# A gated mix of sliding attention and a token MLP on Trainium2: when the first two W2 loads are issued

## The chip, the cores and the metric

The kernel runs on one core of one Trainium2 chip. The metric is the device time of one execution in microseconds (us), taken as the median of several runs. A profiled execution has a time of its own, and its span, from the first to the last instruction of the program, is somewhat shorter than that.

The engines are named as the profile names them: PE (TensorE, matrix multiplications; PEld is its weight load), DVE (VectorE), ACT (ScalarE), POOL (GpSimd) and SP (SyncE, which here only issues transfers). A "q" behind a name, as in SPq, is the sequencer of that engine, where transfers are issued and semaphores are waited for. Every transfer runs on the core's 16 DMA engines. In the profile's table of queues, q1 carries the transfers issued by SP, q10 those by ACT and q0 those by POOL.

## The reference

The inputs are bf16. One token sequence `A_x` of 2048 x 512 goes through two branches that a gate mixes:

```
q, k, v = x @ wqkv                 # 32 heads of 16
a = softmax(q . k[s - 0, 2, .., 14] / 4) . v[s - 0, 2, .., 14] @ wo
h = layernorm(x)
u = gelu(h^T @ w1 + b1)            # contracts 2048 tokens, 1792 features F
b = (u @ w2 + b2)^T                # contracts F, back to 2048 tokens
g = sigmoid(sum(x * gate_w))
out = g * a + (1 - g) * b
```

W1 is 2048 x 1792 and W2 is 1792 x 2048. Both go through the core once.

## The kernel before

Everything lives in one SBUF tensor, `arena`, that is cut into named regions. Regions are used again by other data once their first data is dead, so a load into such a region must wait until the last reader is through.

**The planner.** The kernel does not write its instructions down in order. It collects operations with estimated durations, with the named resources that each reads and writes, and with two kinds of ties to other operations. `deps` is a real dependence: the operation waits until the other has finished, and for a load that means until it has landed. `after` is a tie of order only: the operation comes after the other is issued. A list scheduler (`_pass`) then picks an order for each engine, by earliest possible start and then by the length of the chain of work behind an operation, and `plan_waits` puts a semaphore wait in front of an operation wherever a dependence is not already known to be met. All of this happens when the kernel is built; on the chip each engine runs its list in order, and an instruction that waits holds everything behind it on its own engine.

**The stages on PE.** First the q, k and v projections (L586, L645). Then "phase 2", `ph2_<ft>_<half>` (L853): for each of 14 tiles of 128 features, two halves of eight 512-column matmuls that contract the tokens with W1; GELU on ACT writes the result to `UT`. Two small groups of the attention scores, `sum0` and `sum1` (L709, L714), are placed between them. Then "phase 3", `ph3_<i>_<half>` (L880): for each of 16 output tiles, two halves of seven matmuls with W2, and four more with the attention output and `wo` (L889, five tiles behind). The output tiles are evacuated by ACT (L448, the last half by DVE at L929) and stored by SP (L902, L932).

**The attention beside it.** DVE forms the products of queries and keys and sums them up (L445), with some sums done by accumulating transfers on the POOL queue (L739, L822). After the softmax of each half of the tokens, POOL issues four transfers of 512 KB that spread the attention weights over the partitions, `av0_0` to `av0_3` for the first half and `av1_0` to `av1_3` for the second (L782).

**The weight loads.** All go out on SP through the helper `load`, so all of them stand at L487. W1 comes in seven loads of 1024 KB, `w1_0` to `w1_6`, each for two feature tiles, into three slots that are used in turn (`W1W`, resources `w1s0` to `w1s2`). Load `w1_j` waits until PE has finished with `w1_(j-3)`: `w1_6` goes out when feature tile 7 is done, and feature tile 12 is the first that needs it. W2 comes in eight loads of 896 KB, `w2_0` to `w2_7`, each for two output tiles. They take dead regions: `w2_0` and `w2_1` lie side by side in the region `XT` (the transposed input), `w2_2` to `w2_4` in the W1 slots, `w2_5` and `w2_6` in `X`, and `w2_7` in small softmax buffers. `W2ALIAS[j]` (L370) names the resources that load j overwrites; the helper counts them as written, so a load waits for their readers and for whoever wrote them last.

Two of these ties matter here. The eight loads are chained by `after`, each behind the one before it, and `w2_0` behind `w1_6`; so the SP list goes on `w1_6, w2_0, w2_1, ... w2_7`, and then come the output stores. And `w2_0` and `w2_1` both name all of `XT` (`XTALL`) as written, although each fills its own part of it. Since `w2_0` is then the last writer of `XTALL`, `w2_1` has `w2_0` as a dependence: SP waits until `w2_0` has landed before it issues `w2_1`.

On PE, `ph2_12_0` waits for `w1_6`, `ph3_0_0` for `w2_0`, `ph3_2_0` for `w2_1`, `ph3_4_0` for `w2_2`, and so on. Phase 3 begins with an order written out by hand, `head` (L908): the first halves of tiles 0, 1 and 2, then their second halves.

Of the kernel before, what the change touches and what calls it, by code (L numbers as in the profile page):

```python
# [307 lines left out]
def bass_gated_mix__sliding_local_dilated__mixer_token_mlp__prompt_kernel(nc, A_x, A_wqkv, A_wo, B_x, B_w1, B_b1, B_w2, B_b2, gate_w, out, dbg=None):  # L308
    with contextlib.ExitStack() as es:
# [54 lines left out]
        def w2view(name, extra=0):  # L364
            return view(name, BF16, [(256, NFT), (1, 256)], extra=extra)

        XTALL = ["xt0_%d_%d" % (t, k_) for t in range(4) for k_ in range(2)] + ["xt1", "xt2", "xt3"]
        W2S = [w2view("XT"), w2view("XT", NFT * 256), w2view("W1", NST * 256), w2view("W1", 2 * NST * 256), w2view("W1"),
               w2view("X"), w2view("X", NFT * 256), w2view("S4")]
        W2ALIAS = [XTALL, XTALL, ["w1s1"], ["w1s2"], ["w1s0"],  # L370
                   ["x%d" % t for t in range(7)], ["x%d" % t for t in range(7, 14)], ["s4", "s2", "s1", "rs", "rb"]]
        assert 4 * UT_ * 4 + 2 * UT_ * 4 + 2 * UT_ * 4 + UT_ * 2 >= NFT * 256 * 2
        WO = view("WO", BF16, [(D, 4), (1, D)])
# [104 lines left out]
        w1ld = {}  # L478
        late_dep = [[]]

        def load(name, dst, src, nbytes, writes, transpose=False, queue="sp", issue=0.5, order=True, deps=(), after=()):
            ds = sch.dsem(name)

            def fn(e):
                if transpose:
                    return e.dma_start_transpose(dst, src)
                return e.dma_start(dst, src)  # L487
            op = sch.dma(queue, fn, nbytes, ds, issue=issue, writes=writes, deps=list(deps) + late_dep[0],
                         after=list(after) + ([last_ld[queue]] if order and queue in last_ld else []), name=name)
            if order:  # L490
                last_ld[queue] = op
            return op
# [37 lines left out]

        def ld_w2(j):
            w1ld[7 + j] = load("w2_%d" % j, W2S[j], w2v[:, :, 256 * j:256 * j + 256], F * 256 * 2, ["w2_%d" % j] + W2ALIAS[j], order=False,
                               after=[w1ld[6 + j]])

        ld_w1(0)

# [331 lines left out]
        for j in range(8):  # L868
            ld_w2(j)
# [144 lines left out]
```

## Time and profile before

| | |
|---|---|
| median of 4 runs | 168.63 us (168.23 to 168.94) |
| the profiled execution, own time | 168.23 us |
| its span | 166.5 us |
| PE busy | 160.8 us, 97% of the span, 817 matmuls |
| DVE busy | 150.9 us, 91% |
| ACT busy | 75.2 us, 45% |
| TensorE clock granted | full in all slices |
| bytes moved by DMA | 32.11 MB; q1 21.96 MB, q0 9.45 MB |

How to read it: PE and DVE both have little idle time. An engine's busy share is an average over the stages, so what a change in one place is worth has to be read from the waits in that place. A "time to landing" runs from the issue of a transfer to the last of its 16 semaphore increments, one from each DMA engine that carries a share of it.

### The profile page before, as it was taken

The numbers are of one execution on the slowest core, as the hardware profiler recorded it, in microseconds if no ns is written. First come the engines' busy times: TensorE is split into PE (matmuls) and PEld (weight loads), VectorE is DVE, ScalarE is ACT, GpSimd is POOL, SyncE is SP. The second block draws the span as 40 slices with busy tenths as digits, with TensorE's granted clock in tenths as the row PEclk, the third lists the DMA queues.
The fourth block names the chain that finished last, engine by engine and source line by source line (L and its number), as shares of the span: only waits on it lengthen the run. The fifth ranks groups of instructions, "written<-read, shape, count | busy, mean of one in ns | idle before, by whom it ended". The sixth has DMA issues, their size and how long they took to land.

```text
span 166.5 us, 2019 instructions
## 1 busy us (share of the span) xinstructions
PE 160.8 (97%) x817; PEld 78.7 (47%) x817; DVE 150.9 (91%) x126; ACT 75.2 (45%) x104; POOL 13.7 (8%) x38
## 2 busy tenths in 40 slices
PE   7999999999999999999999599999999999999993
PEld 2765555555544444444444244444444444444742
DVE  0399999999999999999999996999999999999931
ACT  3356677766682799762111639410022211111164
POOL 7000002020000000005000000005001221000000
PEclk9999999999999999999999999999999999999999
DMA  5999997729597082768997749999996899971014
GB/s 167 325 233 265 198 320 134 129 47 189 141 292 218 4 248 60 196 187 136 187 253 247 217 113 303 290 290 290 224 365 230 169 217 184 210 176 37 32 55 134
DMA packets 44120, 32.11 MB, mean 193 GB/s; under 512 B 7248, under 2 KB 41680, under 8 KB 44112
## 3 DMA queue, kind: packets, MB, share of 16 engines
q1 hardware_dynamic: 40800, 21.96, 49.5%
q0 software_dynamic: 2608, 9.45, 27.7%
q10 hardware_dynamic: 704, 0.59, 1.1%
q8 instruction: 6, 0.10, 0.2%
q14 instruction: 2, 0.02, 0.0%
HBM read 18.88 MB, written 2.10 MB: 126 GB/s over the span
## 4 chain that ended last, share of the span: by engine, by line
PE 86%; DMA 10%; POOL 1%; issue 0%; DVE 0%; POOLq 0%
PE ps L880 29%; PE ps L645 23%; PE ps L853 21%; DMA arena<-in_B_w_dram 10%; PE ps L889 8%; PE ps L586 3%; POOL arena L487 1%; PE ps L567 1%; PE ps L709 1%; PE ps L714 1%; PE ps L558 0%; DVE arena L929 0%; POOL arena L455 0%; PE ps L794 0%; POOL arena L454 0%
## 5 line engine op out<-in xcount | busy, mean ns | idle before, releaser
L445 DVE TENSOR_TENSOR arena<-arena 128x4096 bf16<-128x4096 bf16 (+8 forms) x79 | 132.0, 1720 | 2.2 <-ACT arena L448 1.2
L853 PE MATMUL ps<-arena 128*128 128x512 bf16 x224 | 49.0, 379 | 1.8 <-DMA arena<-in_B_w_dram 1.8
L880 PE MATMUL ps<-arena 128*128 128x512 bf16 (+1 forms) x238 | 50.2, 367 | 0.0
L448 ACT ACTIVATE arena<-ps,arena 128x512 bf16<-128x512 f32 (+1 forms) x30 | 21.7, 728 | 61.6 <-PE ps L889 41.5
L448 ACT ACTIVATE arena<-ps 128x512 bf16<-128x512 f32 (+3 forms) x53 | 32.9, 629 | 19.2 <-PE ps L645 11.1
L645 PE MATMUL ps<-arena 128*128 128x512 bf16 x176 | 38.3, 379 | 0.0
L880 PEld LDWEIGHTS ps<-arena 128*128 128x128 bf16 x238 | 23.3, 98 | 25.3
L853 PEld LDWEIGHTS ps<-arena 128*128 128x128 bf16 x224 | 21.7, 98 | 28.4 <-issue 2.7
L645 PEld LDWEIGHTS ps<-arena 128*128 128x128 bf16 x176 | 19.9, 113 | 17.7
L889 PE MATMUL ps<-arena 128*128 128x512 bf16 (+1 forms) x68 | 15.6, 367 | 0.0
L949 ACT ACT_TABLE_LOAD x11 | 14.1, 1283 | 2.5 <-issue 2.3
L782 POOL DMA_DIRECT2D arena<-arena x8 | 4.3, 561 | 75.3 <-DVE arena L445 75.3
L889 PEld LDWEIGHTS ps<-arena 128*128 128x128 bf16 x68 | 6.7, 98 | 7.2
L684 DVE BATCH_NORM_STATS2 arena<-arena 128x6 f32<-128x512 bf16 x16 | 9.8, 683 | 0.0
L448 ACT ACTIVATE arena<-arena 128x16 f32<-128x16 f32 (+5 forms) x10 | 6.8, 679 | 5.7 <-DVE arena L445 5.6
L579 DVE COPY arena<-ps 128x256 bf16<-128x256 bf16 x4 | 1.1, 292 | 5.1 <-PE ps L567 5.1
L698 DVE TENSOR_SCALAR arena<-arena 128x512 bf16<-128x512 bf16 x16 | 5.5, 418 | 0.0
L822 POOL DMA_DIRECT2D arena<-arena x3 | 3.6, 1200 | 19.0 <-DVE arena L445 19.0
L739 POOL DMA_DIRECT2D arena<-arena x2 | 2.5, 1234 | 29.4 <-DVE arena L695 20.7
L929 DVE TENSOR_SCALAR arena<-ps,arena 128x256 bf16<-128x256 f32 x1 | 0.5, 545 | 4.4 <-PE ps L889 4.4
L586 PE MATMUL ps<-arena 128*128 128x256 bf16 x32 | 4.5, 297 | 0.0
L586 PEld LDWEIGHTS ps<-arena 128*128 128x128 bf16 x32 | 3.5, 119 | 1.0 <-DVE arena L579 0.7
(39 smaller groups left out, 20.4 us busy)
## 6 DMA issues: line engine op xcount, KB each, us to landing
arena<-in_B_w_dram SPq DMA_DIRECT2D x7, 1024.0 KB, 6.0
arena<-in_B_w_dram SPq DMA_DIRECT2D x8, 896.0 KB, 10.0
arena<-arena POOLq DMA_DIRECT2D x5, 1024.0 KB, 8.2
arena<-arena POOLq DMA_DIRECT2D x8, 512.0 KB, 13.1
out_dram<-arena SPq DMA_DIRECT2D x15, 128.0 KB, 2.0
arena<-in_A_x_dram SPq DMA_DIRECT2D x3, 512.0 KB, 4.9
arena<-in_A_wqkv_dram SPq DMA_DIRECT2D x2, 512.0 KB, 4.3
arena<-in_A_wo_dram SPq DMA_DIRECT2D x1, 512.0 KB, 9.3
```

Of the source, the lines that this page charges most:

```text
L445: return lambda e: e.tensor_tensor(out=o_, in0=a_, in1=b_, op=op_)
L448: return lambda e: e.activation(out=o_, in_=i_, func=f_, **kw)
L586: ins = e.matmul(ps[:, dl, hb * 256:hb * 256 + 256], lhsT=sub(WQKV, dt * 3 * D + dl, [(4, 128)]), rhs=XT[:, dt, hb * 256:hb * 256 + 256], ...
L645: ins = e.matmul(ps[:, bank, :], lhsT=sub(WQKV, dt * 3 * D + tn * D + dl, [(4, 128)]), rhs=XT[:, dt, sb * 512:(sb + 1) * 512], start=(dt = ...
L684: A("dve", (lambda t_: lambda e: e.bn_stats(out=ST6[:, t_, :], in_=X[:, t_, :]))(t), 0.67, reads=["x%d" % t], writes=["st%d" % t], name="s ...
L698: A("dve", (lambda t_: lambda e: e.tensor_scalar(out=X[:, t_, :], in0=X[:, t_, :], scalar1=col(RSTD, t_), scalar2=col(NMR, t_), op0=ALU.mu ...
L782: prev = sch.dma("pool", (lambda d_, s_: lambda e: e.dma_start(d_, s_))(dst, src), 524288, sch.dsem("av%d_%d" % (h, c)), issue=1.0, reads= ...
L822: sch.dma("pool", (lambda o_, i_: lambda e: e.dma_start(o_, i_, accum_op=ALU.add, max_dma_last_dim=4096))(pw(0, 4), pw(4, 4)), 1800000, sc ...
L853: ins = e.matmul(ps[:, bank, :], lhsT=W1W[:, (ft // 2) % 3, st, 128 * (ft % 2):128 * (ft % 2) + 128], rhs=X[:, st, :], start=(st == 0), st ...
L880: ins = e.matmul(ps[:, bank, 0:c1 - c0], lhsT=W2S[i // 2][:, ft, 128 * (i % 2):128 * (i % 2) + 128], rhs=UT[:, ft, c0:c1], start=(ft == 0) ...
L889: ins = e.matmul(ps[:, bank, 0:c1 - c0], lhsT=OT[:, i // 2, dl, 128 * (i % 2):128 * (i % 2) + 128], rhs=WO[:, dl, c0:c1], start=False, sto ...
L949: e.preload_act_table_set(want)
```

## The change

`w2_0` gets a dependence on `w1_6`: SP issues it only when the last W1 load has landed. `w2_1` no longer names `XTALL` as written, so it has no dependence on `w2_0` any more and is tied to it by order alone: SP issues it right behind `w2_0`. That the old contents of `XT` are dead is still ensured, since `w2_0` is issued after `w1_6`, which waits for feature tile 7 on PE.

```
-        W2ALIAS = [XTALL, XTALL, ["w1s1"], ["w1s2"], ["w1s0"],
+        W2ALIAS = [XTALL, [], ["w1s1"], ["w1s2"], ["w1s0"],
                    ["x%d" % t for t in range(7)], ["x%d" % t for t in range(7, 14)], ["s4", "s2", "s1", "rs", "rb"]]
...
         def ld_w2(j):
             w1ld[7 + j] = load("w2_%d" % j, W2S[j], w2v[:, :, 256 * j:256 * j + 256], F * 256 * 2, ["w2_%d" % j] + W2ALIAS[j], order=False,
-                               after=[w1ld[6 + j]])
+                               after=[w1ld[6 + j]], deps=[w1ld[6]] if j == 0 else [])
```

No instruction is added or removed on any engine but the waits; no transfer changes its size, its source or its destination.

## The prediction

> **What bounds the kernel now.** I read the engine table first, then the chain of waits around the loads, then who waits for whom on PE and SP, then every load by itself in narrow windows, then the DMA traffic by stage.
>
> The page's first line of the engine table:
>
> ```profile
> PE 160.8 (97%) x817; PEld 78.7 (47%) x817; DVE 150.9 (91%) x126; ACT 75.2 (45%) x104; POOL 13.7 (8%) x38
> ```
>
> PE is busy for all but 5.7 of 166.5 us. The change touches only the one late place where PE stands still, which the chain of waits shows (start us, us, what):
>
> ```profile
> 62.44 15.55 PE ps L853 x72
> 78.00 0.02 issue
> 78.01 16.43 DMA arena<-in_B_w_dram
> 94.44 0.14 issue
> 94.57 7.07 PE ps L853 x32
> 101.64 18.13 PE ps L880 x84
> ```
>
> The load issued at 78.01 is `w1_6`; it lands at 94.44, 16.43 us later, and PE takes up feature tile 12 0.13 us after that. Tiles 12 and 13 take 7.07 us, and phase 3 begins at 101.64. What PE lost is in the waits of PE (us in total, times, longest), and what SP waited for between the loads in the waits of SP:
>
> ```profile
> PE ps L853 <- DMA arena<-in_B_w_dram: 1.8, 1, 1.8
> SPq L487 <- DMA arena<-in_B_w_dram: 7.8, 1, 7.8
> ```
>
> The first line is the whole price of the late `w1_6`: 1.8 us. The second is `w2_1` waiting for `w2_0` to land. Next, L487 in narrow windows (one issue's ns three times over, start, then time to landing): `w1_5`; `w1_6` with `w2_0`; `w2_1`; `w2_2`:
>
> ```profile
> L487 SPq DMA_DIRECT2D arena<-in_B_w_dram x1: 368/368/368, 71.1 to 71.1; - x1
> DMA to landing us min/median/max: 5.6/5.6/5.6
> ...
> L487 SPq DMA_DIRECT2D arena<-in_B_w_dram x2: 367/5604/10841, 78.0 to 78.4; - x2
> DMA to landing us min/median/max: 16.4/17.5/18.6
> ...
> L487 SPq DMA_DIRECT2D arena<-in_B_w_dram x1: 367/367/367, 97.0 to 97.0; - x1
> DMA to landing us min/median/max: 5.4/5.4/5.4
> ...
> L487 SPq DMA_DIRECT2D arena<-in_B_w_dram x1: 697/697/697, 97.5 to 97.5; - x1
> DMA to landing us min/median/max: 8.2/8.2/8.2
> ```
>
> A W1 load in a quiet stretch lands after 5.6 us. `w1_6` took 16.4, with `w2_0` issued 0.4 us behind it; that issue stood on SP for 10.84 us, until 89.2. `w2_1` landed in 5.4 us although `w2_2` was issued 0.4 us behind it, and `w2_2` followed at 105.7, some 3.2 us later. So loads of one queue don't share the engines evenly: the first is not slowed, the second comes one transfer later. What slowed `w1_6` is the other queue: four `av0` transfers of 512 KB, issued by POOL from 75.3 to 77.5. Three of them, then the DMA by stage (window, busy time of each engine, clock, DMA share, GB/s):
>
> ```profile
> L782 POOL DMA_DIRECT2D arena<-arena x3: 551/561/566, 75.9 to 76.9; - x3
> DMA to landing us min/median/max: 9.0/13.1/14.3
> ```
>
> ```profile
> 76.00:79.00 3.00, 3.00 (x16) 1.37 (x14) 3.00 (x2) 0.69 (x1) 1.49 (x3) 1.00 0.81 95
> 80.00:83.00 3.00, 3.00 (x16) 1.35 (x15) 3.00 (x2) 0.69 (x1) 0.00 (x0) 1.00 0.93 175
> 91.00:93.00 2.00, 1.77 (x20) 0.52 (x18) 2.00 (x1) 0.86 (x2) 0.00 (x0) 1.00 1.10 323
> 102.00:112.00 10.00, 10.00 (x48) 4.48 (x47) 9.77 (x8) 4.22 (x6) 0.00 (x0) 1.00 1.19 290
> ```
>
> The engines are busy but move only 95 to 175 GB/s while `av0` is under way, and 323 once it is over, at 91.27 (76.9 + 14.3).
>
> **What the Trainium skill says.** "DMA: Bandwidth & Descriptors", section "Queues, rings and completion order": each DMA engine goes round the queues that have work, packet by packet, and takes one queue's descriptors in ring order. The trace agrees: `w2_1` with `w2_2` behind it is not slower than a lone load, and `w1_6` beside `av0` is nearly three times slower. The same page, "Anatomy of one DMA — SWDGE (gpsimd) path": engines don't wait on semaphores, the issuing sequencer does; a transfer (of the POOL path, for which the figure is given) has a fixed part of about 2.0 us. The trace, for SP's path: 5.4 us for one load against 3.16 from landing to landing in the run of W2 loads, so about 2.2 fixed. That is the price of a restart.
>
> **The change part by part.** All times are of the profiled execution: span 166.5, own time 168.23, which is 0.40 below the median of 168.63.
>
> *1. `w2_0` waits for `w1_6`.* The SP list behind it holds `w2_1` to `w2_7` and the stores; none can be issued in the meantime. The issue moves from 78.38 to 94.44 + 0.03 (SP's reaction: `w2_0`'s last increment came at 97.03, `w2_1` went out at 97.05) = 94.47. At 5.40 us, which `w2_1` of the same size took from a standstill, it lands at 99.87 instead of 97.03. PE needs it at 101.64, less 0.13 of reaction: 1.6 us to spare. The cover is feature tiles 12 and 13, 7.07 us that begin with the very landing that releases SP, so it moves along if `w1_6` is earlier or later; 5.4 + 0.1 fits. Cost 0.
>
> *2. `w2_1` right behind.* It goes out at about 94.9 and lands one transfer, 3.16 us, after `w2_0`: 103.03, against 102.45 now. PE needs it at `ph3_2_0`, two half tiles of 1.51 us into phase 3, at 104.66: 1.5 to spare. Cost 0. SP's wait of 7.8 us goes, and its place is taken by one of some 5 us for `w1_6` (89.2, when the issue of `w2_0` now ends, to 94.4), plus the 10.8 of that issue.
>
> *3. The later loads.* All shift by 103.03 - 102.45 = 0.6 us at most. `w2_2` lands at 106.3 and is needed at 101.64 + 9.07 (head) + 3.02 (tile 3) = 113.7; `w2_3` at 109.4, needed at 120.6. `w2_4` stays tied to the end of tile 13 and to the queue ahead of it. `w2_7` waits for DVE in any case (3.0 us of SP wait at 113.2), which swallows the rest. The first store is due on SP at 121.5, long after. Cost 0.
>
> *4. What `w1_6` gains.* Upper bound first: the whole stall, 1.80. But `w2_0`'s issue stood until 89.2, so its bytes can't have moved much before about 90. In the records of semaphore increments the 16 shares of `w1_6` land from 88.14 to 94.44, those of `av0_3` from 85.70 to 91.27 and those of `w2_0` from 94.10 to 97.03. The last engine of `w1_6` thus ended 3.17 us after the last engine of `av0_3`. One engine's share of `w1_6` is 1 MB / 16 = 65.5 KB; at 323 / 16 = 20.2 GB/s that takes 3.2 us. So on the engine that decides, `w1_6` was starved by `av0` and then ran at full pace, with `w2_0` already on the others: nothing is left for `w2_0` to have cost there. It could only have slowed `av0` between 89.3 and 91.3, and at half pace that would be 1.0 us. Lower bound: below 0 is excluded, since no traffic is added ahead of `w1_6`. I take 0.1 and keep 0 to 1.0.
>
> *5. Order.* `w2_1` stays behind `w2_0` by its tie of order, so the chains that the planner weighs keep their lengths; PE's list is fixed by hand but for `sum0`, `sum1` and `t_e`, which need no W2; DVE and ACT work before phase 3 needs none either. I count no reordering.
>
> *Sum:* -0.1 us: 168.1 for the profiled execution, 168.5 for the median. About 0.5% (0.84 us) is what a measurement of this kernel can tell from no change.
>
> **The rivals.**
> *A, faster: `w2_0` does hold up `w1_6`.* For it: they are issued together and land 2.6 us apart, and PE waits for just this. Against it: the full pace above, and `w2_1`'s undisturbed 5.4. If so, all of the 1.80 can go: feature tile 12 starts at 92.77. DVE doesn't cap this; its attention work ends at 159.45 and the matmuls that need it come at 162.1, 2.6 later, and its own wait for ACT (1.2 us) would shrink too. 168.63 - 1.80 = 166.8; half of it, by slowed `av0`, gives 167.6. It decides for faster from 0.84 us on. Chance 0.08.
>
> *B, slower: the two W2 loads share the engines.* With both starting from nothing, and packets of both interleaved, `w2_0` would land with `w2_1`, at 103.03, and PE would stand from 101.64 to 103.17: +1.5 us, 170.1. It costs from a landing time of 7.07 us on, and shows as slower from 7.9. Against it: `w2_1` and `w2_2` were in the same position and came one after the other. Chance 0.06.
>
> *C: the change doesn't do what it says.* Were `w2_1` still to wait for `w2_0`, it would go out at 99.9 and land at 105.3, and PE would lose 105.3 + 0.13 - 104.66 = 0.8 us at `ph3_2_0`: 169.4. By the code no dependence is left. Chance 0.02.
>
> **How the numbers follow.** My forecast, no change within 0.5%, has 0.84. Faster is A, 0.08; slower is B and C together, 0.08 (C's 0.8 us stands at the bound and is counted here). Predicted 168.5. Noise of the median is about 0.3 to each side (the runs span 168.23 to 168.94); the gain's bound of 1.0 pulls the lower end to 167.7, and a C-like loss the upper one to 169.3. The rest of A and B lies outside.
>
> **What would show it.** Right: `w2_0` issued within 0.1 us of `w1_6`'s landing, at about 94.4 and landing in 5.4; `w2_1` 0.4 behind, landing 8.2 after its issue; SP's wait for a load changed in place; PE's wait at L853 still 1.7 to 1.8 us, with none at L880; phase 3 from 101.6. Wrong: a landing time of `w1_6` under 15 us with PE's wait gone (A), or a PE wait for a load at L880 (B, C).

## The result and the profile after

| | before | after |
|---|---|---|
| median | 168.66 us (64 runs) | 168.51 us (43 runs) |
| ratio of after to before, 95% interval | | 1.0004 (0.9987 to 1.0020) |
| profiled execution, own time / span | 168.23 / 166.5 us | 169.39 / 167.6 us |

The time did not change measurably. A second comparison gave 1.0022 (0.9996 to 1.0049). Runs more than 1.5% above the fastest of the same kernel are left out of the ratios. The two profiled executions of the changed kernel (169.39, and 169.49 in the second one) both lie above its median, so what they show in excess of 166.5 us is not the typical run.

The chain of waits of the changed kernel around the loads (start us, us, what), and then the waits of PE and of SP (us in total, times, longest):

```profile
62.42 15.55 PE ps L853 x72
77.98 0.02 issue
77.99 16.49 DMA arena<-in_B_w_dram
94.48 0.14 issue
94.62 3.63 PE ps L853 x16
```

```profile
PE ps L853 <- DMA arena<-in_B_w_dram: 1.9, 1, 1.9
PE ps L541 <- POOL arena L454: 1.1, 1, 1.1
PE ps L889 <- DVE arena L445: 0.6, 1, 0.6
```

```profile
SPq L487 <- DMA arena<-in_B_w_dram: 16.1, 1, 16.1
```

`w1_6` still took 16.49 us, although no transfer stood behind it on its queue any more, and PE's wait at L853 is 1.9 us where it was 1.8. SP's long wait is the new one, for `w1_6`. The loads after the change, in narrow windows of L487: `w1_6`, then `w2_0`, then `w2_0` and `w2_1` together.

```profile
L487 SPq DMA_DIRECT2D arena<-in_B_w_dram x1: 368/368/368, 78.0 to 78.0; - x1
DMA to landing us min/median/max: 16.5/16.5/16.5
...
L487 SPq DMA_DIRECT2D arena<-in_B_w_dram x1: 368/368/368, 94.5 to 94.5; - x1
DMA to landing us min/median/max: 7.1/7.1/7.1
...
L487 SPq DMA_DIRECT2D arena<-in_B_w_dram x2: 368/594/821, 94.5 to 94.9; - x2
DMA to landing us min/median/max: 7.1/8.5/9.9
```

`w2_0` went out at the landing of `w1_6`, as expected, but took 7.1 us, not 5.4. It landed at 101.62; PE took it up at 101.75, with less than 0.1 us of idle time at L880. So the cover of tiles 12 and 13 held, with nothing to spare.

### The profile page after: what moved, and what is told of

Same layout as the page of the kernel before. It is cut to its first block, busy times and chain, and to the rows that moved or that the text cites. A ratio compares the mean times of both kernels' runs of the same rounds, so it can differ in the third digit from the quotient of the medians.

```text
span 167.6 us, 2019 instructions
## 1 busy us (share of the span) xinstructions
PE 160.9 (96%) x817; PEld 78.1 (47%) x817; DVE 151.1 (90%) x126; ACT 75.2 (45%) x104; POOL 13.7 (8%) x38
## 4 chain that ended last, share of the span: by engine, by line
PE 37%; DVE 29%; DMA 22%; SPq 7%; ACT 2%; issue 1%
DVE arena L445 29%; PE ps L853 19%; PE ps L645 16%; DMA arena<-in_B_w_dram 10%; DMA arena<-arena 7%; SPq L486 6%; DMA arena<-in_A_x_dram 5%; ACT arena L448 2%; SPq L487 1%; PE ps L889 1%; ACT L949 1%; PE ps L709 1%; PE ps L714 1%; DVE arena L929 0%; PE ps L794 0%
## 5 line engine op out<-in xcount | busy, mean ns | idle before, releaser
L853 PE MATMUL ps<-arena 128*128 128x512 bf16 x224 | 49.0, 379 | 1.9 <-DMA arena<-in_B_w_dram 1.9
L880 PE MATMUL ps<-arena 128*128 128x512 bf16 (+1 forms) x238 | 50.2, 367 | 0.1
L645 PE MATMUL ps<-arena 128*128 128x512 bf16 x176 | 38.5, 379 | 0.3 <-DMA arena<-in_A_x_dram 0.3
L880 PEld LDWEIGHTS ps<-arena 128*128 128x128 bf16 x238 | 23.1, 98 | 25.8 <-issue 0.5
L853 PEld LDWEIGHTS ps<-arena 128*128 128x128 bf16 x224 | 21.7, 98 | 28.5 <-issue 2.8
L949 ACT ACT_TABLE_LOAD x11 | 14.1, 1283 | 2.5 <-issue 2.3
L586 PE MATMUL ps<-arena 128*128 128x256 bf16 x32 | 4.0, 274 | 0.0
L541 PE MATMUL ps<-arena 128*128 128x512 bf16 x5 | 2.3, 628 | 1.1 <-POOL arena L454 1.1
## 6 DMA issues: line engine op xcount, KB each, us to landing
arena<-in_B_w_dram SPq DMA_DIRECT2D x8, 896.0 KB, 10.1
```

The source lines that it names most:

```text
L586: ins = e.matmul(ps[:, dl, hb * 256:hb * 256 + 256], lhsT=sub(WQKV, dt * 3 * D + dl, [(4, 128)]), rhs=XT[:, dt, hb * 256:hb * 256 + 256], ...
L645: ins = e.matmul(ps[:, bank, :], lhsT=sub(WQKV, dt * 3 * D + tn * D + dl, [(4, 128)]), rhs=XT[:, dt, sb * 512:(sb + 1) * 512], start=(dt = ...
L853: ins = e.matmul(ps[:, bank, :], lhsT=W1W[:, (ft // 2) % 3, st, 128 * (ft % 2):128 * (ft % 2) + 128], rhs=X[:, st, :], start=(st == 0), st ...
L880: ins = e.matmul(ps[:, bank, 0:c1 - c0], lhsT=W2S[i // 2][:, ft, 128 * (i % 2):128 * (i % 2) + 128], rhs=UT[:, ft, c0:c1], start=(ft == 0) ...
L949: e.preload_act_table_set(want)
```

## The experiments

**The theory** was that the four `av0` transfers of POOL hold up `w1_6`, that `w2_0` has no part in it, and that the added wait lies under tiles 12 and 13. **Rival A**: `w2_0` shares the blame. **Rival B**: two W2 loads in flight slow each other. "Ratio" is always to the kernel before on the same chip, with its 95% interval.

**1. The changed kernel again.**

> The changed kernel again, for a second profile beside the kernel before on the same chip. Theory (the POOL transfers av0 hold w1_6 up, w2_0 has no part in it; the wait is covered by feature tiles 12 and 13): w1_6 still takes about 16.4 us to land, PE still waits 1.7 to 1.9 us at L853; w2_0 goes out within 0.1 us of that landing and lands 5.1 to 5.5 us later, with 1 us or more to spare before phase 3; time 0.0 +- 0.3 us against before. Rival A (w2_0 shares in holding up w1_6): w1_6 lands in under 15.5 us, PE's wait under 1 us, 1 to 1.8 us faster. Rival B (the two W2 loads share the engines and are late): a PE wait for a load at L880 of about 1.5 us, 1.5 us slower.

Ratio 1.0022 (0.9996 to 1.0049). `w1_6` took 16.9 us and PE waited 2.3 us at L853 (tile 11 had ended earlier in this execution). `w2_0` landed 6.6 us after its issue, at 101.02. No wait at L880. A and B both miss; the space before phase 3 was 0.5 us, not the 1 us that I had asked for.

**2. The alias alone.** The other edit is left out:

```
-        W2ALIAS = [XTALL, XTALL, ["w1s1"], ...
+        W2ALIAS = [XTALL, [], ["w1s1"], ...
```

> One half of the change alone: w2_1 no longer names XTALL, w2_0 still goes out right behind w1_6. So three loads stand in SP's queue while av0 is under way. Theory (loads of one queue are served in order): w1_6 lands after 16.4 us as before, w2_0 about 2.6 us behind it at 97.0, w2_1 about 3 us behind that, near 100.1 instead of 102.4; PE's wait at L853 1.7 to 1.9 us; time 0.0 +- 0.3 us. Rival A: with one more load beside it, w1_6 lands later than 17 us and PE waits over 2.4 us, 0.6 us slower or more.

Ratio 1.0008 (0.9986 to 1.0031). `w1_6` 16.7 us with two loads behind it, `w2_0` at 97.5, `w2_1` at 100.5; PE's wait 2.1 us. Two loads queued behind `w1_6` don't slow it by more than single executions scatter: with nothing behind it, it took 15.3 to 16.9 us in five of them.

**3. The wait alone.** `w2_0` waits for `w1_6`, and `w2_1` still waits for `w2_0`:

```
-                               after=[w1ld[6 + j]])
+                               after=[w1ld[6 + j]], deps=[w1ld[6]] if j == 0 else [])
```

> The other half alone: w2_0 waits for w1_6 to land, and w2_1 still waits for w2_0 to land. This is rival C of the prediction made real. Theory: w2_0 lands at 99.9, w2_1 goes out then and lands 5.4 us later at 105.3; PE needs it at 104.66, so a new PE wait of 0.6 to 0.9 us stands at L880 and the time is 0.6 to 0.9 us above before. Rival D (the space of 1.5 us behind w2_1 is larger than the modelled matmul ends suggest, or a restart costs less than 2.2 us): no wait at L880, time unchanged.

I was right about the place and wrong about the size. Two of six runs came out near 170 (169.86 and 171.09), the other four at 176.6 to 179.3; the median of all six is 177.21, 5.3% above before (168.34). The ratio of 1.0147 (1.0080 to 1.0215) counts only the two near 170. What decides between the two outcomes was not tried, but the long times have a cause in the kernel: the next experiment has them in every run. The waits of PE in one of the long runs here:

```profile
PE ps L880 <- ACT arena L448: 7.2, 1, 7.2
PE ps L880 <- DMA arena<-in_B_w_dram: 1.7, 1, 1.7
```

The second line is the wait that I expected, for `w2_1` (landed at 105.37). The first, four times as long, was in nobody's expectation.

**4. A longer wait.** The changed kernel, with `w2_0` held until feature tile 12 is done:

```
-                ... deps=[w1ld[6]] if j == 0 else [])
+                ... deps=[w1ld[6], ph2op[12, 1]] if j == 0 else [])
...
-                PE(f_ph2(ft, bank, half), 1.735, ...
+                ph2op[ft, half] = PE(f_ph2(ft, bank, half), 1.735, ...
```

> The changed kernel with the wait made longer: w2_0 waits for w1_6 and also for the end of feature tile 12 on PE, some 3.6 us after the landing; w2_1 right behind it. Measures the space that the change has. Theory: w2_0 goes out at about 98.2 and lands at 103.6; PE needs it at 101.6, so PE waits about 2.1 us at L880; w2_1 lands at 106.8 and is needed 3.0 us after phase 3 begins at 103.7, so it costs nothing or 0.2 more. Time 1.9 to 2.4 us above before, about 170.7. Rival B (the loads share the engines): both land at about 106.8, a PE wait of about 5 us at L880, time about 173.8.

Ratio 1.0582 (1.0524 to 1.0640), median 178.26: nearly five times the cost that I expected. The loads themselves did what they should (`w2_0`, then `w2_1`, in windows of L487):

```profile
L487 SPq DMA_DIRECT2D arena<-in_B_w_dram x1: 368/368/368, 98.3 to 98.3; - x1
DMA to landing us min/median/max: 5.2/5.2/5.2
...
L487 SPq DMA_DIRECT2D arena<-in_B_w_dram x1: 822/822/822, 98.7 to 98.7; - x1
DMA to landing us min/median/max: 7.9/7.9/7.9
```

`w2_0` landed 5.2 us after its issue and `w2_1` 3.2 us behind it: B is out. The rest is in the waits of PE and ACT, and in the first store (L902):

```profile
PE ps L880 <- ACT arena L448: 6.1, 1, 6.1
PE ps L880 <- DMA arena<-in_B_w_dram: 1.9, 1, 1.9
```

```profile
ACT arena L448 <- DMA out_dram<-arena: 15.9, 1, 15.9
```

```profile
L902 SPq DMA_DIRECT2D out_dram<-arena x1: 5127/5127/5127, 127.2 to 127.2; - x1
...
who waited for it (us, times):
  ACT arena L448: 15.9, 1
...
DMA to landing us min/median/max: 24.0/24.0/24.0
```

Then `w2_7`, the load ahead of this store on SP, and last the same store in the kernel before:

```profile
L487 SPq DMA_DIRECT2D arena<-in_B_w_dram x1: 11111/11111/11111, 116.0 to 116.0; - x1
...
DMA to landing us min/median/max: 34.8/34.8/34.8
```

```profile
L902 SPq DMA_DIRECT2D out_dram<-arena x1: 361/361/361, 121.5 to 121.5; - x1
...
DMA to landing us min/median/max: 7.7/7.7/7.7
```

Read from below. The store of output tile 0 went out at 127.2 (before: 121.5) and landed 24.0 us later (before: 7.7). ACT's evacuation of tile 4 writes the same output buffer, since the ring has four, so it waited 15.9 us for that landing. PE needs a PSUM bank (a part of the memory that the matmuls write to) that this evacuation frees, and waited 6.1 us. The store was late twice over because it stood behind `w2_7`. On SP, the issue of `w2_7` lasted from 116.0 for 11.1 us. On the queue, `w2_7` landed at 150.80, 34.8 us after its issue (before: 14.1), and the store 0.36 us behind it, at 151.16; from about 113 on POOL's `av1` and then its accumulating transfers were under way. And there is a third part, in the clock row of the page (one digit for each fortieth of the span):

```profile
PEclk9999999999999999999999999999999998589999
```

With PE's stop the granted clock fell: it was 0.79 from 145.5 to 152.0, mostly the stop itself, and 0.61 from 152.0 to 157.2. (The clock records have half the full clock from 149.25 to 156.08.) The 14 matmuls after the stop took 5.15 us; 14 such matmuls take 3.02 in the chain of the kernel before, so 2.1 us were lost. The parts sum to 1.9 + 6.1 + 2.1 = 10.1 us, and the span is 176.8 - 166.5 = 10.3 longer.

**5. The same, with eight output buffers.** To tell whether the ring of four is what makes it so dear:

```
-            A("act", act(OUTS[:, i % 4, :], ...
+            A("act", act(OUTS[:, i % 8, :], ...
```

The stores, their semaphores and the resources go with it in the same way; the buffers take the room of two dead softmax buffers and one new slot.

> The kernel whose w2_0 waits until feature tile 12 is done (5.8% above before, where 1.2% was expected), with eight output buffers in the ring instead of four (in the room of two dead softmax buffers and one new slot), so that ev4 no longer waits for the store of tile 0. Theory (the late W2 loads push w2_7 and the first stores behind it into the accumulating transfers of POOL; the store of tile 0 lands some 24 us late; the ring of four makes ACT and then PE wait for it, and PE loses its clock on top): the store of tile 0 still lands late, near 150, but ACT doesn't wait for it before tile 8; PE's wait of 6 us for ACT and the granted clock of 0.98 are gone; PE's wait of 1.9 us for w2_0 stays; time 1.0 to 2.0% above before, 170 to 171.5. Rival (the extra time comes from elsewhere, such as a slower PE after the wait for w2_0): still 4% or more above before.

Ratio 1.0131 (1.0089 to 1.0172), median 170.12. The waits of PE, and the first store:

```profile
PE ps L880 <- DMA arena<-in_B_w_dram: 2.0, 1, 2.0
PE ps L853 <- DMA arena<-in_B_w_dram: 1.8, 1, 1.8
PE ps L541 <- POOL arena L454: 1.1, 1, 1.1
```

```profile
L902 SPq DMA_DIRECT2D out_dram<-arena x1: 11065/11065/11065, 128.1 to 128.1; - x1
...
DMA to landing us min/median/max: 24.2/24.2/24.2
```

The store is as late as before, 24.2 us, and now nobody waits for it: ACT's wait for a store, PE's wait for ACT and the lower clock are all gone, and what is left is the wait for `w2_0`. So it is the ring of four that turns the late store into the extra 8 us (medians of 178.26 and 170.12, on two chips on which the kernel before has 168.34 and 168.09).

**6. `av0` out of the way.** The kernel before, with one wait more on POOL and no other edit: `av0_1`, and in order `av0_2` and `av0_3`, go out only when `w1_6` has landed. The wait is put in after planning, so no order changes (`avop` is a list that collects the four transfers as they are made):

```
-        sch.plan_waits()
+        sch.plan_waits(); avop[0][1].waits.append(w1ld[6])
```

> The kernel before, with one wait more on POOL: av0_1 (and in order av0_2 and av0_3 behind it) goes out only when w1_6 has landed. av0_0 alone stays ahead. Takes away three quarters of the suspected cause. Theory (av0 starves w1_6): w1_6 waits for av0_0 alone and lands after 6 to 8 us, at about 85, PE's wait of 1.8 us at L853 is gone and tile 12 starts at 92.8; av0_1 to av0_3 land by about 98, av0_1 before DVE wants it at 104; w2_0 shares the engines with them, lands by 99 and is needed at 99.7; the time falls by 1.5 to 1.8 us (about 1%), DVE ending 2.6 us ahead of its last readers does not cap it. Rival A (w2_0, issued right behind w1_6, holds it up): w1_6 still lands after 15 us or more, no gain. Rival E (the stall only moves: w2_0, starved by av0 in w1_6's place, comes late): w1_6 lands early, but a new PE wait for a load stands at L880, gain under 0.5 us.

Ratio 0.9991 (0.9964 to 1.0019). `w1_6` landed after 8.1 us with `w2_0` right behind it, and PE's wait at L853 was gone. That is the theory, and A is out: `w2_0` was still issued right behind it. But the gain was taken back as E had it, one load later than E had said:

```profile
PE ps L880 <- DMA arena<-in_B_w_dram: 1.2, 1, 1.2
```

```profile
L487 SPq DMA_DIRECT2D arena<-in_B_w_dram x1: 368/368/368, 89.4 to 89.4; - x1
DMA to landing us min/median/max: 15.1/15.1/15.1
```

`w2_0` landed at 89.3, ahead of the released `av0_1` to `av0_3`. `w2_1`, which here still waits for `w2_0`, went out at 89.4 behind them and took 15.1 us, in the very place that `w1_6` had held.

**7. The same wait in the changed kernel.**

> The same added wait on POOL, in the changed kernel: when w1_6 lands, w2_0 on SP and av0_1 on POOL are released together. Theory: w1_6 lands at about 85 as in the kernel before with this wait; w2_0 then starts beside av0_1 to av0_3 and is starved until they are through, landing at 97 to 100 where it is needed at 99.7; the time falls by 1.0 to 1.8 us, at most as much as without the change. Rival A: holding w2_0 back helps w1_6, so this one is faster than the same kernel without the change by 0.5 us or more.

Ratio 0.9903 (0.9882 to 0.9924), median 166.17. The one wait that PE has left, and `w1_6`:

```profile
PE ps L541 <- POOL arena L454: 1.1, 1, 1.1
```

```profile
L487 SPq DMA_DIRECT2D arena<-in_B_w_dram x1: 368/368/368, 77.7 to 77.7; - x1
DMA to landing us min/median/max: 8.6/8.6/8.6
```

It is faster than experiment 6 by 0.9%. That was A's mark, but A's mechanism is not there: `w1_6` landed no sooner (8.6 us against 8.1). What differs is `w2_1`, which lands at 100.3 instead of 104.5, so that PE no longer waits for it. `w2_0` came at 94.9, earlier than I had expected. Which half of the change it takes is not told by this run; the next pair tells it.

**8. Which half is worth something, once `av0` is held.** The kernel before with the alias edit alone and the wait on POOL, and experiment 7 once more beside it:

> The kernel before with av0_1 to av0_3 held on POOL until w1_6 has landed, and the alias half of the change alone: w2_0 goes out right behind w1_6 and w2_1 right behind w2_0, both ahead of the held transfers. Tells which half of the change is worth something once av0 is out of the way (with no half: span 166.5, a PE wait of 1.2 us for w2_1; with both: 164.3, no wait). Theory (the useful half is that w2_1 doesn't wait for w2_0; the wait on w1_6 has no use): w1_6 lands at about 86.5, w2_0 at about 89.3, w2_1 before 100, no PE wait for a load; time 0.8 to 1.1% below before, equal to the kernel with both halves within 0.3%. Rival (the wait on w1_6 is the useful half): w1_6 lands later or a PE wait of 0.5 us or more for a load is left; at most 0.5% below before.

> Both halves of the change with av0_1 to av0_3 held until w1_6 has landed, once more, beside the kernel with the alias half alone on the same chip. Theory: 0.8 to 1.1% below before again, no PE wait for a load, within 0.3% of the kernel with the alias half alone. Rival (the wait on w1_6 is the useful half): faster than that one by 0.5% or more.

Alias alone 0.9906 (0.9870 to 0.9943), both halves 0.9904 (0.9875 to 0.9934); spans 164.6 and 164.7, and in both PE waits for no load of W1 or W2. So the alias alone is worth as much as both: `w2_1` must not wait for `w2_0`. The wait on `w1_6` adds nothing that can be measured.

**9. Half of `av0` out of the way.** As 6, but only `av0_2` and `av0_3` are held (`avop[0][2]`):

> The kernel before, with av0_2 and av0_3 (not av0_1) held on POOL until w1_6 has landed: half of the suspected cause taken away. Theory: av0_0 and av0_1 are through by about 84, w1_6 lands at 86 to 88, after 8.5 to 10 us, before PE wants it at 92.8; the wait at L853 is gone; av0_2 and av0_3 are through by 97, w2_0 lands by 99; the time falls by 1.5 to 1.8 us. Rival A: w1_6 lands after 15 us or more, no gain. Rival E: a new PE wait for w2_0 at L880.

Ratio 0.9955 (0.9927 to 0.9982); span 164.6 with no PE wait for W1 or W2. `w1_6` landed after 11.2 us, a miss of my 8.5 to 10. The gain is 0.75 us, half of what I expected, though the profiled execution was 1.9 us shorter than the one before. Its DVE waits 1.5 us for an accumulating transfer, which 7 and 8 don't show; whether that explains the rest was not tried.

With four, two and one of the `av0` transfers ahead of it `w1_6` took 16.4, 11.2 and 7.5 to 8.6 us (four profiles), and with none, like `w1_5`, 5.6. With four that is 2.7 us for each. The packet records show how. In the first profile of the changed kernel, where `w1_6` was alone on SP's queue, 170 of its packets started between 82 and 86, and 184 data packets of `av0`; in the second profile it was 200 and 176. The numbers are similar, but a packet of `w1_6` has 512 bytes and one of `av0` 4096: in the first profile `w1_6` got 22 GB/s and `av0` 188.

## Why the prediction was right or wrong

The forecast, no change (168.5 predicted, 168.51 measured), was right, and for the main reason that it gave: `w2_0` has no measurable part in the late `w1_6`. Part of it was luck, since the space that it counted on behind the wait was mostly used up. By its steps:

- **Step 4, what `w1_6` gains.** Right. Taken at 0.1 us with 0 to 1.0 kept; measured, `w1_6` took 16.5 and 16.9 us with nothing behind it (15.3, 16.2 and 16.4 in experiments 3, 4 and 5), 16.3 on average, against 16.4 with one load and 16.7 with two. One execution, the 15.3 of experiment 3, would fit the upper bound of 1.0; the five together don't. Rival A is out, and experiments 6, 7 and 9 show `av0` as the cause. The step's argument took the last share of `av0_3` and that of `w1_6` to be on one engine; the records don't name the engine of a share, so that part stays open.
- **Step 1, `w2_0` waits.** The cost of 0 was right, the term under it was not. A landing time of 5.40 us from a standstill left 1.6 us to spare; in the two profiled executions it was 7.1 and 6.6, and 0.0 to 0.5 us was left. That it cost nothing there was luck. In the records of semaphore increments 15 of the 16 shares had landed by 100.05 (99.59 in the second execution) and one came at 101.62 (101.02). The packet records show one packet of 16,384 bytes on the queue that the profile's page calls "instruction", started at 95.58 and lasting 1.80 us (95.91, 1.25 us), just as the bytes of `w2_0` began to move. Experiment 3 has the same picture (packet at 94.57, lasting 1.92 us; 15 shares of `w2_0` by 98.33, the last at 100.12). Where `w2_0` went out later (experiments 4 and 5, at 98.3 in the former), its 16 shares landed within 0.6 us. In the kernel before, the same packet at 95.57 met the tail of `w2_0`, for which nobody but SP was waiting. The agreement in time is shown in these runs; that the packet is the cause is not, since it was not moved. The Trainium skill, "Runtime: NRT & Kernel Launch", section "Instruction fetch mechanics", says that an engine's instructions are refilled in blocks of 16 KiB by a DMA queue of their own; the packet's size agrees.
- **Step 2, `w2_1` right behind.** It landed 3.16 us behind `w2_0`, the predicted distance, so at 104.78 and 104.19 instead of 103.03. PE, with phase 3 begun at 101.75, didn't wait.
- **Step 3, the later loads.** The shift of 0.6 us was mis-sized, and the sentence that `w2_7`'s wait for DVE "swallows the rest" is the step that failed. The chain came some 2 us late, most of it step 1's late `w2_0` (`w2_1` 1.2 to 1.75 us behind its forecast). In the first profile `w2_6` landed at 128.25 (before: 118.21), `w2_7` 20.1 us after its issue at 113.6 (before: 14.1 after 113.2), the first store took 12.2 us instead of 7.7, and DVE waited 3.4 us for an accumulating transfer, after which PE waited 0.6. The store, and DVE's wait:

```profile
L902 SPq DMA_DIRECT2D out_dram<-arena x1: 5991/5991/5991, 121.8 to 121.8; - x1
...
DMA to landing us min/median/max: 12.2/12.2/12.2
```

```profile
DVE arena L445 <- DMA arena<-arena: 3.4, 1, 3.4
```

The median doesn't show it, so whether a typical run has this loss is not known. What I had missed is, by these times, that a load on SP that is still under way when POOL fills the engines, from 113 on, comes many microseconds late, and everything behind it on SP with it.
- **Rival C's price** of 0.8 us was far too small. Made real in experiment 3, it cost 8 to 11 us in four runs of six (176.6 to 179.3 against 168.34) and 1.5 to 2.8 in the other two; the long ones went through the first store, the ring of four buffers, ACT, PE and its clock. C itself didn't happen, but the profiled executions of the changed kernel are not far from that case: their `w2_1` landed at 104.8 and 104.2 and their `w2_7` was issued at 113.6 and 113.2, against 105.4 and 115.4 in the long run of experiment 3. Where between them the edge lies was not measured. The range would not have held that case; a rival of that kind was missing from the text.
- **Step 5, order.** Right: the instructions of every engine stand in the same order in both kernels.
- **SP's wait.** Right. Expected as some 5 us plus the 10.8 us of the issue that stood, in place of 7.8; measured as 16.1 in one piece.

## What to carry to other kernels

Before you hold a transfer back to help another, ask whose bytes the late one is really waiting for: a load behind it on the same queue cost it nothing measurable here, while four transfers of another queue cost 2.7 us each. Holding three of them back gained 1%, but only together with freeing the next load from a wait that an over-broad list of overwritten buffers had put there; holding two back gained 0.45% without that. And follow a shift of a load to the end of its issuing queue: PE waited less than 2 us for the late loads themselves (experiments 3 and 4), but `w2_7` and the first store, late behind them, cost up to 10 us at the output ring.

## What the runs showed of the hardware

- The end of one load can hang on one of its 16 shares. In three profiles in which a 16 KB packet of the instruction queue, 1.25 to 1.92 us long, ran as the load began, the last share came 1.4 to 1.8 us behind the other 15. In the changed kernel the loads queued behind kept that offset (in the second profile 102.75 for 15 shares of `w2_1` and 104.19 for the last; 105.91 and 107.37 for `w2_2`).
- Two queues that share the DMA engines got similar numbers of packets, not of bytes: 170 of 512 bytes and 184 of 4096 in the same 4 us, 22 GB/s against 188. The load of 1 MB with the small packets, which lands in 5.6 us alone, took 16.5.
- A stop of PE can cost more than its length. After 6.1 us without work the granted clock was 0.61 over the next 5.2 us, which cost 2.1 us more. After the stop of 1.9 us, in the same run, the profile shows no lower clock. The Trainium skill, "TensorE: Matmul & The Clock Gate", section "Part 1: The HAM clock gate (the "warmup" mystery)", has the array drop to half its clock after an idle window of about 3.4 us; the two stops lie on either side of that and agree; the clock records have the drop 3.3 us into the long stop.
- A store of 128 KB took 24.0 us to land when it was issued at 127.2, behind a load that itself took 34.8 us beside POOL's transfers, and 7.7 us when issued at 121.5, behind one that took 14.1. In both cases it landed soon after that load: 0.36 and 1.8 us.
